# Applying k^T v to q for the later batches: six 32x64 tiles of the matrix array against four 32x128 tiles with a lent PSUM bank

## The chip, the cores and the metric

The kernel runs on one core of a Trainium2 chip. The metric is device time in microseconds, from the run of the whole program; the median of three runs before the change is 1015.61 us (1014.79 to 1016.51). The engines are named as the profile names them: PE is TensorE's matmuls and PEld its weight loads, DVE is VectorE, ACT is ScalarE, POOL is GpSimd, and SP is the engine that issues most DMAs.

## The reference

Two blocks, all in float32. The first is an attention without softmax, over 8 batches, 8 heads, 576 tokens and a head size of 64; the second is a gated feed-forward layer on its output, 4608 tokens of 512 values.

```python
kv = np.einsum('bhsd,bhse->bhde', k, v)
out = np.einsum('bhsd,bhde->bhse', q, kv)
rms = np.sqrt(np.mean(out * out, axis=-1, keepdims=True) + 1e-06)
attn = out / rms * g_norm
x = attn.transpose(0, 2, 1, 3).reshape(B * S, H * D)
gate = 1.0 / (1.0 + np.exp(-(x @ w_gate)))
return gate * (x @ w_val) @ w_out
```

Below, u is the product of q and k^T v (the `out` of the third line), before the norm.

## The kernel before

**Chunks and batches.** The feed-forward layer works in nine chunks of 512 tokens. Chunk 0 is done with plain matmuls while the weights are converted. Chunks 1 to 8 use a fast scheme with fewer products: the first layer (`first_layer_fast`, PE line L949) has 78 products, numbered p = 0 to 77, in three blocks j of 26 (i = p mod 26); the second layer (L1053) has 26. A product of the first layer is two matmuls of a 128x256 moving operand, and each float32 matmul shows as two records in the trace, so it has four records.

**Attention, hidden in the chunks.** Batch 0 is computed before everything else. Batch b (1 to 7) is computed by `feed(b)` while chunk b - 1 runs: its steps are hung behind numbered products, by a list written out by hand for batch 1 (`places`) and lists of pairs (place, step) for batches 2 to 7 (`first`). "At p" below means: right after product p, on each engine behind what that product issued. Each engine works in the order in which instructions were issued to it.

**The steps of a batch.** `kv_mm` (L376, L382) makes k^T v of all heads in PSUM; `kv_copies` (L387) is twelve ACT copies of 32 partitions into `kvq`. q comes in by `load_q`, a pair of heads at a time, on SP's queue, and `turn` (L393) transposes blocks of 32x32 on DVE into `qTs`, on 96 partitions. `two_pairs` then serves four heads: `u_mm` (L422) is 72 matmuls with weights of 32 partitions and 64 columns (64 tokens) from `qTs` and 64 moving columns from `kvq`; six of them that follow each other lie in six places of the array, three row groups by two column halves. They write a three-bank PSUM tile, `at`. `u_square` (ACT, L428) squares u into `sqs`, `u_sum` (DVE, L431) sums, `u_root` (ACT, L434) takes the root, `u_norm` (DVE, L440) divides u, read from PSUM, and `x_turn` (DVE, L447) transposes back and sends the result into the ring `xT` by DMAs on SP (L457). Batch 1 normalizes on ACT instead (`norm`, L463).

**PSUM.** Of the eight banks, `at` holds three. The products of chunks 1 to 8 share the other five through a queue, `free`: a product that opens a new region takes the front bank, and the bank goes to the back when the region's last reader has been issued. Regions are written more than once. The first layer's list starts so (name of the region, two operands, and what `combine` does after the product):

```python
PRODUCTS1 = (("A", 8, 4, ""), ("B", 18, 10, ""), ("C", 9, 1, ""), ("E", 23, 12, "o5=A"), ("A", 24, 14, "o4=C"),
             ("C", 26, 16, "o3=B o1=A"), ("B", 25, 19, "o1=o1+B"), ("A", 33, 9, "t9=E t9=t9+A t8=C"),
```

`o5=A` is an ACT copy of region A (L915). The product i = 4 adds onto A, so on PE it has to wait until that copy has read A; the product i = 5 adds onto C and waits for `o4=C`; the product i = 6 adds onto B and waits for `o3=B`. Sums such as `o1=o1+B` are on DVE (L919). The lines that order all this for one product:

```python
combine(o, regions, steps, nc.vector if j == N3 - 1 and i == NPR - 1 else nc.gpsimd)
give_all(regions, LAST1, i)
for step in at.get(p, ()):
    step()
```

In chunk 1 the first `u_mm` is at p = 25 and the second at p = 53; in chunks 2 to 6 they are at p = 28 and p = 54 (blocks j = 1 and j = 2, behind i = 2). `u_square` of chunks 2 to 6 is at p = 30 and p = 56, behind the copies `o5=A` and `o4=C`.

Of the kernel before, what the change touches and what calls it, by code (L numbers as in the profile page):

```python
# [10 lines left out]
FP32 = mybir.dt.float32  # L11
# [9 lines left out]
def kernel(  # L21
# [30 lines left out]
    NQ = NP // QB  # L52
    QC = QB * NJ
    NC = HD // QB
    XC = QB * JH
# [38 lines left out]
    def load_q(n):  # L94
        if n >= B * NHP:
            return
        b, h0 = n // NHP, 2 * (n % NHP)
        if n < NE:
            t = first.tile([NP, NJ, 2, HD], FP32, tag="q", name="q")
            for e in range(2):  # L100
                nc.sync.dma_start(out=t[:, :, e, :], in_=q[b, h0 + e].rearrange("(p j) d -> p j d", j=NJ))
        else:
            if b == 1:
                i = n - NE
                t = h_main[2 - i // 2].rearrange("p s c -> p (s c)")[0:NP, (i % 2) * 2 * NJ * HD:(i % 2 + 1) * 2 * NJ * HD]
                t = t.rearrange("p (h c) -> p h c", h=2)
            else:
                t = sb.tile([NP, 2, NJ * HD], FP32, tag="q", name="q", bufs=1)
            nc.sync.dma_start(out=t, in_=q[b, h0:h0 + 2].rearrange("h (p j) d -> p h (j d)", j=NJ))
        pairs[n]["q"] = t  # L110
# [147 lines left out]
    kvq = const.tile([P, NHP, 2 * NC, HD], FP32, name="kvq")  # L258

    qTs = const.tile([P, 2, 2 * NJ * HD], FP32, name="qTs")  # L260
    sqs = const.tile([P, 2 * NU * P], FP32, name="sqs")
    xTs = const.tile([P, NC, 2, S // 2], FP32, name="xTs")
# [15 lines left out]
    def attention(n, at_ps):  # L278
# [3 lines left out]
        kv = kvq[:, m, 0]  # L282
# [19 lines left out]
        def q_out():  # L302
            d["qT"] = qTs[:, n % 2, 0:S]
            nc.scalar.copy(out=d["qT"].rearrange("p (i n) -> p i n", i=2), in_=d["q"][:, :, 0:JH * NP])
# [59 lines left out]
    def feed(b):  # L364
# [20 lines left out]
        def kv_copies(i, rs):  # L385
            for r in rs:
                nc.scalar.copy(out=kvq[QB * r:QB * r + QB, :, i].rearrange("p (s n) d -> p s n d", s=2),  # L387
                               in_=d["kv"][QB * i:QB * i + QB])

        def turn(n, e):  # L390

            w_ = NJ * HD
            nc.vector.transpose(qTs[0:NP, n % 2, w_ * e:w_ * e + w_],  # L393
                                pairs[n]["q"][:, e].rearrange("p (j i c) -> p i j c", i=NC, c=QB))
            if e == 1:
                if b > 1:
                    load_q(n + 1)
                elif n == 2 * NHP - 1:
                    load_q(n + 1)

        def two_pairs(n0):


            d = {}
            ms = sb.tile([P, NQ, NJ], FP32, tag="ms2", name="ms2", bufs=1)
            sq = sqs[:, 0:2 * S].rearrange("p (r c) -> p r c", r=NQ)
            units = [slice(NJ // 2 * i, NJ // 2 * (i + 1)) for i in range(2)]

            def by_head(t):
                return t.rearrange("p r (n d) -> p r n d", d=HD)  # L410

            def u_mm(some=range(2)):
                if 0 in some:
                    d["u"] = at_ps()[:, 0:NQ, 0:2 * QC]
                u = d["u"]
                for which in some:
                    for g in range(JH):
                        for i in range(NC):
                            for r in range(NQ):
                                for e in range(2):  # L420
                                    c, o = NJ * HD * e + QC * i + PH * g, HD * (JH * which + g)
                                    nc.tensor.matmul(u[HD * e:HD * e + HD, r, o:o + HD],  # L422
                                                     qTs[QB * r:QB * r + QB, (n0 + which) % 2, c:c + PH],
                                                     kvq[QB * r:QB * r + QB, (n0 + which) % NHP, NC * e + i],
                                                     start=(i == 0), stop=(i == NC - 1))

            def u_square():
                nc.scalar.activation(out=sq, in_=d["u"], func=AF.Square)  # L428

            def u_sum(i):  # L430
                nc.vector.tensor_reduce(out=ms[:, :, units[i]], in_=by_head(sq)[:, :, units[i]], axis=AX.X, op=ALU.add)  # L431
# [4 lines left out]
            def u_norm(i):  # L436
                if i == 0:
                    nc.vector.reciprocal(ms, ms)
                m_ = ms[:, :, units[i]]
                nc.vector.tensor_tensor(out=by_head(sq)[:, :, units[i]], in0=by_head(d["u"])[:, :, units[i]],  # L440
                                        in1=m_.unsqueeze(3).to_broadcast([P, NQ, NJ // 2, HD]), op=ALU.mult)

            def x_turn(i):


                for which in range(2):
                    nc.vector.transpose(xTs[:, i, which],  # L447
                                        sq.rearrange("p r (w g i c) -> p w i r g c", w=2, g=JH, i=NC)[:, which, i])
                m = n0 % NHP
                for j in range(2):  # L450
                    for e in range(2):
                        p0, p1 = HD * e + QB * j, HD * e + QB * i
                        s0 = 0
                        while s0 < S // 2:
                            o = (S * b + S // 2 * j + s0) % (NX * G)
                            n_ = min(NX * G - o, S // 2 - s0)
                            nc.sync.dma_start(out=xT_ring[p1:p1 + QB, m:m + 2, o:o + n_],  # L457
                                                          in_=xTs[p0:p0 + QB, i, :, s0:s0 + n_])
                            s0 += n_

            def norm(r):
                for n in range(NJ):
                    nc.scalar.activation(out=by_head(sq)[:, r, n], in_=by_head(d["u"])[:, r, n], func=AF.Copy,  # L463
                                         scale=ms[:, r, n:n + 1])

            if b == 1:
                u_mms = [lambda: u_mm((0,)), lambda: u_mm((1,))]
                norms = [lambda: nc.vector.reciprocal(ms, ms)] + [lambda r=r: norm(r) for r in range(NQ)]
            else:
                u_mms = [u_mm]  # L470
                norms = [lambda: u_norm(0), lambda: u_norm(1)]
            return (u_mms + [u_square, lambda: u_sum(0), lambda: u_sum(1), u_root] + norms +
                    [lambda i=i: x_turn(i) for i in range(NC)])

        def turns_of(n):
            return [lambda n=n, e=e: turn(n, e) for e in range(2)]

        n0 = NHP * b
        kv = [kv_mm] + [lambda i=i: kv_copies(i, range(3)) for i in range(2 * NC)]
        t0, t1, t2, t3 = (turns_of(n0 + i) for i in range(4))  # L480
        u0, u1 = two_pairs(n0), two_pairs(n0 + 2)
# [700 lines left out]
```

## Time and profile before

| What | Before |
|---|---|
| median of three runs | 1015.61 us (1014.79 to 1016.51) |
| span of the profiled execution | 1013.2 us |
| PE busy | 1003.4 us (99%), 6982 records |
| DVE, ACT, POOL busy | 723.7, 360.2, 591.6 us |
| granted TensorE clock | 1.000 over the span |
| `u_mm` (L422) | 2016 records, 26.4 us busy |
| `kv_copies` (L387) | 84 copies, 30.6 us busy |
| `xT<-xTs` on SP (L457) | 128 DMAs |

The profiled execution lists its span only. The median stands 2.4 us over it, and this is taken as what lies around the span. A row of a group view gives the line, engine, names of the tiles, shapes and count, then busy time and mean time of one; a row of a timeline gives start, duration, engine, line, names and count of merged records, and in brackets the idle time before it and what ended it. A "(x144)" there counts records, two for each float32 matmul.

### The profile page before, as it was taken

What the parts mean: (1) busy time and instruction counts of PE and PEld (TensorE: products, weight loads), DVE (VectorE), ACT (ScalarE), POOL (GpSimd) and SP (SyncE); (2) the same over time, 40 slices, a digit from 0 to 9 for tenths busy, and PEclk for the clock granted to TensorE, in tenths of its full rate; (3) what the DMA queues carried; (4) which work ended last, traced back from release to release, by engine and by line L of the source; (5) the groups of instructions that cost most, each with busy time, mean ns of one, the idle gap of its engine ahead of it and who ended that gap; (6) DMA issues with size and microseconds to landing.
All of it is one profiled execution on the core that took longest, in us unless ns stands there. A gap on an engine that the chain in (4) does not pass through costs nothing.

```text
span 1013.2 us, 18540 instructions
## 1 busy us (share of the span) xinstructions
PE 1003.4 (99%) x6982; PEld 824.1 (81%) x6982; DVE 723.7 (71%) x1215; ACT 360.2 (36%) x639; POOL 591.6 (58%) x965
## 2 busy tenths in 40 slices
PE   9999999999999999999999999999999999999998
PEld 8454447888888888888888888888888888888887
DVE  4888998899668856775677666866688556755672
ACT  4568522442144304441354115421453033213320
POOL 0000999898448642966177706962496439744963
PEclk9999999999999999999999999999999999999999
DMA  9796415644688467646766476556664545444514
GB/s 273 237 282 198 151 43 177 216 137 152 209 272 309 165 192 260 221 160 200 238 230 195 147 248 234 191 164 192 229 217 153 179 155 209 162 154 159 211 58 123
DMA packets 100248, 195.07 MB, mean 193 GB/s; under 512 B 24224, under 2 KB 73248, under 8 KB 100160
## 3 DMA queue, kind: packets, MB, share of 16 engines
q0 software_dynamic: 20976, 112.87, 32.8%
q1 hardware_dynamic: 72016, 78.94, 25.4%
q10 hardware_dynamic: 7168, 2.10, 0.9%
q8 instruction: 55, 0.90, 0.4%
q14 instruction: 33, 0.27, 0.1%
HBM read 160.04 MB, written 25.56 MB: 183 GB/s over the span
## 4 chain that ended last, share of the span: by engine, by line
PE 74%; POOL 2%; issue 0%; DVE 0%; POOLq 0%
PE mm L949 47%; PE mm L1053 24%; PE at L422 2%; PE at L376 1%; POOL h L724 1%; POOL w_ring L1024 0%; POOL h_more L724 0%; PE at L382 0%; POOL w L772 0%; DVE sg L919 0%; POOL w L1024 0%; POOLq L1024 0%
## 5 line engine op out<-in xcount | busy, mean ns | idle before, releaser
L949 PE MATMUL mm<-xs,w 128*128 128x256 f32 x1428 | 332.0, 380 | 0.0
L949 PEld LDWEIGHTS mm<-xs,w 128*128 128x128 f32 x1428 | 270.4, 190 | 37.4 <-DVE temps L919 0.4
L949 PE MATMUL mm<-xT,w 128*128 128x256 f32 x948 | 230.0, 380 | 0.0
L949 PEld LDWEIGHTS mm<-xT,w 128*128 128x128 f32 x948 | 179.4, 190 | 25.5 <-issue 1.0
L919 DVE TENSOR_TENSOR sg<-sg,mm 128x512 f32<-128x512 f32 (+1 forms) x176 | 100.8, 599 | 96.0 <-PE mm L949 45.6
L772 POOL DMA_DIRECT2D w<-kept x84 | 46.9, 558 | 190.8 <-PE mm L949 188.5
L1053 PE MATMUL mm<-w,h 128*128 128x256 f32 x630 | 143.4, 379 | 0.9 <-POOL h L911 0.5
L1053 PEld LDWEIGHTS mm<-w,h 128*128 128x128 f32 x630 | 119.5, 190 | 17.9 <-POOL h L911 0.9
L915 ACT COPY temps<-mm 128x512 f32<-128x512 f32 (+1 forms) x128 | 66.0, 537 | 190.0 <-PE mm L949 94.9
L911 POOL TENSOR_TENSOR h<-h,sg 128x512 f32<-128x512 f32 x72 | 97.7, 1374 | 54.0 <-DVE h L919 33.8
L724 POOL TENSOR_TENSOR h<-h 128x128 f32<-128x128 f32 x216 | 114.0, 540 | 16.5 <-DVE h_more L724 13.1
L1053 PE MATMUL mm<-w,h_more 128*128 128x256 f32 x474 | 108.2, 379 | 0.0
L908 ACT ACTIVATE sg<-sg 128x512 f32<-128x512 f32 x96 | 59.6, 630 | 131.5 <-DVE sg L919 131.5
L1053 PEld LDWEIGHTS mm<-w,h_more 128*128 128x128 f32 x474 | 90.1, 190 | 12.2
L915 ACT COPY sg<-mm 128x512 f32<-128x512 f32 (+1 forms) x112 | 57.1, 510 | 91.2 <-PE mm L1053 45.2
L589 PE MATMUL mm<-xT,w 128*128 128x512 f32 x176 | 78.4, 598 | 1.8 <-ACT xT L352 1.5
L724 POOL TENSOR_TENSOR h_more<-h 128x128 f32<-128x128 f32 x120 | 59.1, 495 | 33.5 <-DVE h L911 29.2
L919 DVE TENSOR_TENSOR temps<-temps,mm 128x512 f32<-128x512 f32 (+1 forms) x96 | 59.2, 617 | 25.8 <-PE mm L1053 17.2
L919 DVE TENSOR_TENSOR temps<-mm,temps 128x512 f32<-128x512 f32 (+1 forms) x64 | 39.8, 622 | 51.0 <-PE mm L1053 23.6
L915 ACT COPY h<-mm 128x512 f32<-128x512 f32 x48 | 28.1, 586 | 125.5 <-PE mm L949 110.3
L743 POOL TENSOR_TENSOR h_more<-w 128x256 f32<-128x256 f32 x10 | 12.1, 1231 | 100.7 <-DMA st<-in_moe_w_out_dram 100.7
L919 DVE TENSOR_TENSOR sg<-mm,sg 128x512 f32<-128x512 f32 (+1 forms) x64 | 39.6, 618 | 43.2 <-PE mm L1053 21.8
(135 smaller groups left out, 1313.6 us busy)
## 6 DMA issues: line engine op xcount, KB each, us to landing
w<-kept POOLq DMA_DIRECT2D x42, 896.0 KB, 5.0
w<-kept POOLq DMA_DIRECT2D x90, 384.0 KB, 4.6
w<-kept POOLq DMA_DIRECT2D x42, 768.0 KB, 5.3
out_dram<-sg SPq DMA_DIRECT2D x119, 64.0 KB, 1.7
h_more<-in_k_dram SPq DMA_DIRECT2D x28, 256.0 KB, 5.0
h_more<-in_v_dram SPq DMA_DIRECT2D x28, 256.0 KB, 5.2
q<-in_q_dram SPq DMA_DIRECT2D x24, 288.0 KB, 3.2
xT<-xTs SPq DMA_DIRECT2D x96, 72.0 KB, 3.9
```

Source lines behind the costliest of these rows:

```text
L376: nc.tensor.matmul(ps[HD * e:HD * e + HD, n // 2, n % 2], mains[n, "k"][:, c], mains[n, "v"][:, c], start=(n % 2 == 0 and j == 0), stop=Fa ...
L422: nc.tensor.matmul(u[HD * e:HD * e + HD, r, o:o + HD], qTs[QB * r:QB * r + QB, (n0 + which) % 2, c:c + PH], kvq[QB * r:QB * r + QB, (n0 + ...
L589: nc.tensor.matmul(self.ps[i], w[("wg", "wv")[i], self.f][:, m, :], xT[self.c][:, m, :], start=(m == 0), stop=(m == NMT - 1), skip_group_c ...
L724: ops.append((eng, lambda v=v, x=x, sign=sign, y=y, eng=eng: eng.tensor_tensor(out=h_form(v, j), in0=h_form(x, j), in1=h_form(y, j), op=op ...
L743: nc.gpsimd.tensor_tensor(out=w1_slot(j, w_at[v]), in0=w1_slot(j, w_at[x]), in1=w1_slot(j, w_at[y]), op=op_of(sign))
L772: nc.gpsimd.dma_start(out=granule(g)[:, 0:n], in_=kept1[g // NPA % N3, g % NPA][:, 0:n])
L908: nc.scalar.activation(out=o["o" + step[1]], in_=o["o" + step[1]], func=AF.Sigmoid)
L911: mult.tensor_tensor(out=o[x], in0=o[x], in1=o[y], op=ALU.mult)
L915: nc.scalar.copy(out=o[out_], in_=o[expr])
L919: tt(out=o[out_], in0=o[x], in1=o[y], op=ALU.add if sign == "+" else ALU.subtract)
L949: nc.tensor.matmul(regions[name][1][:, g], ws[:, g], xf[c][wv], start=(new and g == 0), stop=True, skip_group_check=True)
L1053: nc.tensor.matmul(regions[name][1], h_form(hv, j), ws[:, j], start=(used[i] and j == 0), stop=(j == N3 - 1), skip_group_check=True)
```

## The change

For batches 1 to 7 the four heads of a run lie on 32 partitions each, all 128 partitions in use. q of four heads comes in one DMA (`load_q_run`), and `turn` is two transposes of 128x576 for four heads. `u_mm` takes 128 tokens as weights (32 partitions by 128 columns), in five slices of which the last overlaps the one before, so it has 40 matmuls: for each slice and each half of the head size, four that follow each other, one on each row group. They write four banks: the three of `at`, and one more, which is bank 4 for batch 1 and is taken from the queue `free` for batches 2 to 7. For these, a new step `u_copy` has ACT copy u (960 and 320 values a partition) to `sqs` in SBUF, and the bank is given back to the queue when the copies are issued. `u_square` reads the copy and writes into `qTs`; `u_norm` works in SBUF. `kv_copies` is eight copies of 32x128 a batch. `x_turn` is one transpose of 128x640 per half, with twice the number of DMAs of half the size. Tokens come out in another order, and `store` follows it. The places of the steps are new lists: `u_copy` stands with `u_mm` (p = 25, 53 in chunk 1; 28, 54 in chunks 2 to 6), `u_square` at 26, 55 and 30, 56. In chunks 2 to 6 the turns of q move to p = 4, 8, 33, 39; the norms of the first run are at 42 and 44 and its `x_turn` at 47 and 49.

```diff
+        if b == 1:
+            t = h_main[2 - m].rearrange("p s c -> p (s c)")[:, 4 * NT * P - JR * HD:4 * NT * P]
+        else:
+            t = sb.tile([P, JR * HD], FP32, tag="q", name="q", bufs=1)
+        nc.sync.dma_start(out=t, in_=q[b, HR * m:HR * m + HR].rearrange("h (p j) d -> (h p) (j d)", j=JR))
...
-        def kv_copies(i, rs):
-            for r in rs:
-                nc.scalar.copy(out=kvq[QB * r:QB * r + QB, :, i].rearrange("p (s n) d -> p s n d", s=2),
-                               in_=d["kv"][QB * i:QB * i + QB])
+        def kv_copies(e, i):
+            for r in range(2):
+                p0, p1 = HD * e + QB * i, QB * (2 * r + e)
+                nc.scalar.copy(out=kvq[p1:p1 + QB, :, i], in_=d["kv"][p0:p0 + QB, :, r])
+
+        def turn(m, i):
+            nc.vector.transpose(qTs[:, S * i:S * i + S],
+                                q_late[b, m].rearrange("p (j i c) -> p i j c", i=NC, c=QB)[:, i])
...
+            un = sqs.rearrange("p (h s d) -> p h s d", h=HR, d=HD)
+            sq = un if b == 1 else qTs.rearrange("p (h s d) -> p h s d", h=HR, d=HD)
...
+            def u_mm():
+                d["bank"] = None if b == 1 else free.popleft()
+                more = bank(4 if b == 1 else d["bank"])
+                at = at_ps()
+                d["u"] = [by_slice(at[:, 0:NAT]), by_slice(more.unsqueeze(1))]
+                for s_ in range(NSL):
+                    c = min(P * s_, S - P)
+                    for i in range(NC):
+                        for h in range(HR):
+                            nc.tensor.matmul(d["u"][h // NAT][:, h % NAT, s_],
+                                             qTs[QB * h:QB * h + QB, S * i + c:S * i + c + P],
+                                             kvq[QB * h:QB * h + QB, m, i],
+                                             start=(i == 0), stop=(i == NC - 1))
+
+            def u_copy():
+                nc.scalar.copy(out=un[:, 0:NAT], in_=d["u"][0])
+                nc.scalar.copy(out=un[:, NAT:HR], in_=d["u"][1])
+                give(d["bank"])
...
             def u_square():
-                nc.scalar.activation(out=sq, in_=d["u"], func=AF.Square)
+                if b == 1:
+                    nc.scalar.activation(out=sq[:, 0:NAT], in_=d["u"][0], func=AF.Square)
+                    nc.scalar.activation(out=sq[:, NAT:HR], in_=d["u"][1], func=AF.Square)
+                else:
+                    nc.scalar.activation(out=sq, in_=un, func=AF.Square)
...
+                nc.vector.transpose(xTs[:, i].rearrange("p h c -> p (h c)"),
+                                    sqs.rearrange("p (h s i c) -> p i (h s) c", h=HR, i=NC, c=QB)[:, i])
...
-            return (u_mms + [u_square, lambda: u_sum(0), lambda: u_sum(1), u_root] + norms +
+            return ([u_mm] + ([u_copy] if b > 1 else []) + [u_square, lambda: u_sum(0), lambda: u_sum(1), u_root] + norms +
                     [lambda i=i: x_turn(i) for i in range(NC)])
...
+        names = ("t00 t01 t10 t11 u0 c0 q0 s00 s01 r0 n00 n01 x00 x01 u1 c1 q1 s10 s11 r1 n10 n11").split()
+        steps_ = dict(zip(names, t0 + t1 + u0 + u1[:8]))
+        where = """0:t00 5:t01 25:u0,c0 26:q0 28:s00 30:s01 31:t10 35:t11 42:r0 46:n00 48:n01 50:x00 52:x01 53:u1,c1
+                   55:q1 57:s10,s11 60:r1,n10 62:n11""" if b == 2 else """
+                   4:t00 8:t01 28:u0,c0 30:q0,s00 32:s01 33:t10 37:r0 39:t11 42:n00 44:n01 47:x00 49:x01 54:u1,c1
+                   56:q1,s10,s11 60:r1 61:n10 63:n11"""
...
     def at_ps():
-        return psum.tile([P, NQ, 512], FP32, tag="at", name="at")
+        return psum.tile([P, NAT, 512], FP32, tag="at", name="at")
```

## The prediction

> **What bounds the kernel now.** I read the busy times first, then TensorE's waits, then the groups of small matmuls, then the timelines of PE, ACT and DVE around one `u_mm`.
>
> ```profile
> PE 1003.4 (99%) x6982; PEld 824.1 (81%) x6982; DVE 723.7 (71%) x1215; ACT 360.2 (36%) x639; POOL 591.6 (58%) x965
> ```
>
> The waits of TensorE over the span come to some 6 us, most of it at the start; one of them matters later:
>
> ```profile
> PE mm L949 <- ACT sg L915: 0.8, 1, 0.8
> ```
>
> So PE sets the end: whatever lengthens PE's work, or makes it wait, lengthens the kernel by as much. The groups of small matmuls and weight loads:
>
> ```profile
> L422 PE MATMUL at<-kvq,qTs 32*64 32x64 f32 x2016 | 26.4, 224 | 0.4 <-ACT sqs L463 0.3
> ...
> L949 PEld LDWEIGHTS mm<-xs,w 128*128 128x128 f32 x1428 | 270.4, 190 | 37.4 <-DVE temps L919 0.4
> L422 PEld LDWEIGHTS at<-kvq,qTs 32*64 32x64 f32 x2016 | 24.1, 130 | 7.6 <-issue 5.4 <-ACT sqs L463 1.1 <-ACT cz L206 0.8
> L376 PEld LDWEIGHTS at<-h_more 128*64 128x64 f32 x448 | 13.6, 138 | 3.2 <-issue 2.4 <-ACT sg L594 0.8
> ```
>
> A load of 64 columns takes 130 ns with 32 rows and 138 with 128 rows, one of 128 columns 190: rows hardly count, and 64 more columns cost 52 ns, 0.81 ns a column. The timeline of PE in chunk 2:
>
> ```profile
> 288.05 2.09 PE L376 MATMUL at<-h_more 128*64 128x64 f32 x64
> 290.06 0.46 PE L382 MATMUL at<-h_more 64*64 64x64 f32 x16
> ...
> 294.88 1.03 PE L949 MATMUL mm<-xs,w 128*128 128x256 f32 x4
> 295.74 1.03 PE L949 MATMUL mm<-xT,w 128*128 128x256 f32 x4
> 296.69 1.85 PE L422 MATMUL at<-kvq,qTs 32*64 32x64 f32 x144
> 298.48 4.58 PE L949 MATMUL mm<-xs,w 128*128 128x256 f32 x20
> ```
>
> A product comes every 0.86 us (294.88 to 295.74). With `u_mm` between, the next comes after 2.74, and its first load adds 0.10 (4.58 against 4 x 0.86 + 1.03), so one `u_mm` costs 1.98 us. Of the twelve in chunks 1 to 6 the mean is 1.98. L376's 64 records are 32 rounds of two tiles: (2.09 - 0.27) / 31 = 58.5 ns a round. L382's 16 are four rounds of four tiles in 0.46, the same pace, and the 144 here are 24 rounds of six. A round of 64-column loads thus takes 58.5 ns whatever the number of tiles, and tiles in different rows load side by side. ACT and DVE there:
>
> ```profile
> 296.14 1.24 ACT L915 COPY h<-mm 128x512 f32<-128x512 f32 x2
> 298.58 1.13 ACT L428 ACTIVATE sqs<-at 128x1152 f32<-128x1152 f32 x1 [1.19 <-PE at L422]
> 299.61 0.58 ACT L915 COPY sg<-mm 128x512 f32<-128x512 f32 x1
> ```
>
> ACT makes `o5=A` and `o4=C` (296.14) before `u_mm` ends, then waits for u. In chunk 4, VectorE before the second `u_mm` (536.37):
>
> ```profile
> 531.25 0.26 DVE L438 RECIPROCAL ms<-ms 128x18 f32<-128x18 f32 x1
> 531.54 0.76 DVE L440 TENSOR_TENSOR sqs<-at,ms 128x576 f32<-128x576 f32 x1
> 532.21 0.56 DVE L393 STREAM_TRANSPOSE qTs<-q 96x384 f32<-96x384 f32 x1
> 532.71 0.72 DVE L440 TENSOR_TENSOR sqs<-at,ms 128x576 f32<-128x576 f32 x1
> 533.35 0.67 DVE L919 TENSOR_TENSOR sg<-mm,sg 128x512 f32<-128x512 f32 x1
> ...
> 535.73 0.68 DVE L919 TENSOR_TENSOR h<-mm,temps 128x512 f32<-128x512 f32 x1
> 536.34 1.54 DVE L447 STREAM_TRANSPOSE xTs<-sqs 128x288 f32<-128x288 f32 x4
> ```
>
> VectorE has no gap here. The operation that ends at 536.41 is the last reader of the bank at the front of `free` at that moment.
>
> **The change part by part.**
>
> *`u_mm` on PE.* 40 matmuls in rounds of four, two records each: 20 rounds. Each row group loads 128 columns a round: 0.81 x 128 = 104 ns, plus the 5 to 6 ns by which a 64-column round exceeds its load (58.5 against 53), so 109. Rounds: 20 x 0.109 = 2.18. The rest of `u_mm` (changing over on both sides, the first load) is 0.58 now (1.98 - 24 x 0.0585); L376 with L382, read in the same way, gives 0.50 with one change-over more, of 0.15. I take 0.40, first long load included: 2.58, or 0.60 more each. Twelve: +7.2. In batch 1 each run has two half `u_mm` of 1.18 (62.66 to 63.65 and the edges), and one of 2.58 replaces them: +0.2 each, +0.4. Bounds: a round at the old 58.5 (1.57 in all), and load and move one after the other (0.107 + 0.053 = 0.163 a round, 3.66). The load rows are the nearest, so 109.
>
> *`u_copy` on ACT.* The rows for copies and squares (586 ns for 512 values, 1131 for 1152) give 0.85 ns a value over 150: 968 ns for 960 values, 423 for 320, 1240 for the square; the next may start some 0.105 before an end. In chunks 2 to 6 `u_copy` is issued at p = 28 and 54, ahead of `o5=A` and `o4=C`, and waits for the end of `u_mm`, so both copies, early now, queue behind it. From that end: copies start at 0.03 and 0.89, `o5=A` at 1.21 to 1.80, `o4=C` to 2.28, the square 2.17 to 3.41, `o3=B` 3.30 to 3.89. PE runs product i = 3 from 0.04, then i = 4 would start at 0.89, but writes A: it starts at 1.80 + 0.05, and its load is no longer hidden (0.10): 1.96, a wait of 1.07. Product i = 5 is in time (C read at 2.28, due 2.82); i = 6 needs B, read at 3.89, and would be due at 3.68: 0.37 more. So 1.44 each, ten times: +14.4. In chunk 1, at p = 25, four products stand between and nothing waits; at p = 53 the same sum gives 0.2 and 0.75, less the 0.8 of the wait shown above, which is of this kind and goes: +0.2. Bounds for the ten: 0, and 2.3 each if the square also delayed i = 5.
>
> *The lent bank and VectorE.* The fourth tile of `u_mm` now waits for the front bank's last reader. At p = 28 two turns that stood at p = 24 are gone, and nothing waits. At p = 54 VectorE has, ahead of that reader, a reciprocal, two norms of 640 values (0.75 each, from the 0.76 for 576) and two transposes of 640 (446 ns for 288 and 559 for 384 give 0.86, every 0.80): 3.4 us where 531.25 to 533.35 has 2.1. The reader ends 1.3 later, at 537.7; `u_mm` is due at 536.28 and waits till then: 1.3 in five chunks, +6.5. Bounds: 0 (VectorE catches up) and 2.0.
>
> *Batch 1.* Norms on ACT go from 18 to 20 (one every 0.2), squares from one to two: the wait of the second run for `at` (0.3 now, on L463) grows by some 0.5: +0.5.
>
> *At nothing.* ACT's `kv_copies` (84 of 364 ns, then 56 shorter) end before `u_mm`. Turns are half as many and longer (0.79 for 576 values), beside PE. q's loads: one for two, issued 20 products ahead. DMAs into `xT`: 240 for 128, 0.6 us each on SP; 16 last some 10 us where 8 took 5.9, and behind them SP's stores wait; the sums that read them begin about 12 us after the first, so they end just in time. If that cover failed, each chunk lost 1 to 2 us of VectorE, and the banks there have about 3 us to spare.
>
> *Sum*: 7.2 + 0.4 + 14.4 + 0.2 + 6.5 + 0.5 = +29.2. Against the profiled span: 1013.2 + 29.2 = 1042.4; with the 2.4 around it, **1044.8 us**.
>
> **The rivals.**
>
> *Copies in time (chance 0.15).* PE meets neither ACT's queue nor the bank, only its own work: +8.1, 1023.7. For it: ACT is busy 36%. Against: the order of issue, and the 0.8 wait.
>
> *Short loads (0.10).* The 32x128 load is no slower than the 64-column one: `u_mm` 1.57, so -0.41 x 12 and -0.8 a run in batch 1, -6.5 in all; the other terms stay: +15.1, 1030.7. Against: 190 against 138 ns. The Trainium skill, page "TensorEngine Tiling (Array Packing)", section "Restrictions", says that column tiling shuts off Fast Weight Load, and the change drops column tiling; but the skill's page "TensorE: Matmul & The Clock Gate", section "Weight-path perf modes", gives that mode to weights that are not float32 only. No run so far shows a 32x128 load.
>
> *Load and move in turn (0.06).* A row group cannot load while it multiplies: `u_mm` 3.66, +1.68 x 12 and +2.6 in batch 1; +22.8 and the others' 21.6: 1060. Against: four records of L949, each with a 128-column load of about 0.10 and 256 moving columns, come in 0.86. The Trainium skill, page "TensorE: Matmul & The Clock Gate", section "The mechanism", says that a load overlaps running matmuls only when its row group differs, which would give this rival's time; these four records, all on the full array, disagree.
>
> *Absorbed (0.07), the other side.* PE is not the true bound of a chunk, and what it loses in the first layer comes back at the layers' ends, where it would otherwise wait for POOL's sums of h. Price nil: 1015.6, the median of before. It decides if a chunk can give back 29.2 / 6 = 4.9 us. Against: in chunks 1 to 6 (182 to 812 us) PE is busy 628.25 of 630.
>
> **How the numbers follow.** The forecast has 0.62 and by itself 1035 to 1053, from its three bounds taken by halves. 1022 to 1054 takes in the first two rivals and leaves out some 2 in 10, the last two with the tails. 0.2% is 2 us, about what a measurement of this kernel can tell from no change. Faster 0.03 and same 0.03 are the last rival's, with 0.01 slower; slower 0.94.
>
> **What would show it.** `u_mm` as 1120 records in about 2.6 us each, with loads near 184 ns; `PE mm L949` waiting for ACT's copies at L921 of the changed file (`h`, then `sg`), ten times near 1.1 and ten near 0.4; PE in `u_mm` waiting for DVE's `h` once a chunk. Wrong, if `u_mm` stays at or under 2 us, if PE has no wait at i = 4, or if PE's idle time grows by less than 10 us.

## The result and the profile after

The changed kernel takes 1042.6 us (median of four runs, 1042.15 to 1043.99) against 1015.2 of the kernel before: a ratio of 1.0269, 95% interval 1.0256 to 1.0281. The span of its profiled execution is 1040.7 us against 1013.2, so 27.5 us have to be found. Times below are medians of four runs too, but for `order_all`: one run of it took 3787.8 us, which nothing here explains, and its time is the median of the other three. The busy times of the page:

```profile
PE 1019.1 (98%) x6086; PEld 830.8 (80%) x6086; DVE 720.2 (69%) x1159; ACT 358.6 (34%) x641; POOL 593.2 (57%) x965
```

PE is busy 15.7 us longer with 896 records fewer, and the rest is time in which it stands still. What it stands still for (reason, us in total, times, longest):

```profile
PE mm L955 <- ACT h L921: 8.1, 11, 0.8
...
PE mm L425 <- DVE h L925: 1.4, 5, 0.3
...
PE mm L955 <- DVE sg L925: 0.9, 1, 0.9
```

L955, L921 and L925 are L949, L915 and L919 of before, and L425 is the new `u_mm`. These sums are too small, since products overlap: the next is due 0.16 us before the record of the one ahead ends (0.97 behind its start, where the row lasts 1.13), and the load that a wait lays bare costs 0.10 more. So I took the starts of the products in both traces (both have 3744 records of the first and second layer, in the same order) and subtracted: how much later does product p + 1 start after product p than it did before?

| Place | Before to after, us | How often | Sum, us |
|---|---|---|---|
| `u_mm` itself (the product behind it) | 2.74 to 3.35: 0.61 | 12 | 7.3 |
| i = 4 and its load, behind the first `u_mm` | 0.98 + 0.10 | 5 | 5.4 |
| i = 4 and its load, behind the second | 0.84 + 0.10 | 5 | 4.7 |
| i = 6 and its load, behind both | 0.30 + 0.10 | 10 | 4.0 |
| second `u_mm`, beyond the 0.61 | 0.76 in four chunks, 0.40 in chunk 4 | 5 | 3.4 |
| product p = 50 and its load | 0.23 in four chunks, 1.21 in chunk 2 | 5 | 2.1 |
| chunk 1, the rest (0.58 of it at p = 78, the first product of the second layer, a wait for POOL) | | 1 | 0.5 |
| batch 1 (0.1), start (-0.25), small ones (0.3), end (-0.2) | | | -0.1 |
| sum (of 27.5) | | | 27.3 |

Elsewhere products start as far apart as before; chunks 7 and 8, in which no attention runs, have no difference at all.

The groups of `u_mm` by tile, from the view of that line (duration least, median, greatest in ns; then the forms):

```profile
L425 PE MATMUL at<-kvq,qTs x840: 270/270/318, 62.4 to 779.1; 32*128 32x64 f32 x168
L425 PE MATMUL mm<-kvq,qTs x280: 270/270/318, 62.4 to 779.3; 32*128 32x64 f32 x140
```

```profile
L425 PEld LDWEIGHTS at<-kvq,qTs x840: 181/187/187, 62.4 to 779.1; 32*128 32x128 f32 x168
```

A load of 32 rows and 128 columns takes 187 ns, within 3 ns of the 190 of a 128x128 load before. The starts of the 80 records of one `u_mm` come as 7, 6, 7, then 92 ns: four records close together, then a pause, 111 or 112 ns a round (160 for the first).

PE and ACT behind the first `u_mm` of chunk 2 (start, duration, engine, line):

```profile
300.79 1.13 PE L955 MATMUL mm<-xs,w 128*128 128x256 f32 x4
302.74 4.12 PE L955 MATMUL mm<-xs,w 128*128 128x256 f32 x16 [0.82 <-ACT h L921]
```

```profile
300.91 0.96 ACT L431 COPY sqs<-at 128x960 f32<-128x960 f32 x1 [4.27 <-PE mm L425]
301.76 0.43 ACT L432 COPY sqs<-mm 128x320 f32<-128x320 f32 x1
302.08 1.09 ACT L921 COPY h<-mm 128x512 f32<-128x512 f32 x2
303.04 1.30 ACT L440 ACTIVATE qTs<-sqs 128x1280 f32<-128x1280 f32 x1
304.21 1.09 ACT L921 COPY sg<-mm 128x512 f32<-128x512 f32 x2
```

ACT waits 4.27 us for `u_mm` with `o5=A` and `o4=C` queued behind the copies (the x2 at 302.08), and `o3=B` (304.21) behind the square. Product i = 3 starts at 300.79, i = 4 at 302.74, just after the first of the two has read A. The 16 records from there take 4.12 us, 0.5 more than four products that follow each other without a wait: 0.10 is the load that the wait at i = 4 laid bare, 0.40 is i = 6 with its load.

VectorE and PE around the second `u_mm` of chunk 2:

```profile
322.28 0.84 DVE L456 STREAM_TRANSPOSE xTs<-sqs 128x640 f32<-128x640 f32 x1
323.04 0.65 DVE L925 TENSOR_TENSOR sg<-mm,sg 128x512 f32<-128x512 f32 x1
323.62 0.82 DVE L456 STREAM_TRANSPOSE xTs<-sqs 128x640 f32<-128x640 f32 x1
...
326.13 0.68 DVE L925 TENSOR_TENSOR h<-mm,temps 128x512 f32<-128x512 f32 x1
```

```profile
321.62 1.13 PE L955 MATMUL mm<-xs,w 128*128 128x256 f32 x4 [0.95 <-DVE sg L925]
...
326.87 0.32 PE L425 MATMUL mm<-kvq,qTs 32*128 32x64 f32 x1 [0.28 <-DVE h L925]
```

The fourth tile, in the lent bank, starts when the sum at 326.13 has ended. And a product five places earlier, p = 50, already waits for a sum that VectorE does late.

### The profile page after: what moved, and what is told of

Same layout as the page of the kernel before. It is cut to its first block, busy times and chain, and to the rows that moved or that the text cites. A ratio compares the mean times of both kernels' runs of the same rounds, so it can differ in the third digit from the quotient of the medians.

```text
span 1040.7 us, 16813 instructions
## 1 busy us (share of the span) xinstructions
PE 1019.1 (98%) x6086; PEld 830.8 (80%) x6086; DVE 720.2 (69%) x1159; ACT 358.6 (34%) x641; POOL 593.2 (57%) x965
## 4 chain that ended last, share of the span: by engine, by line
PE 66%; DVE 4%; ACT 4%; issue 1%; POOL 1%; DMA 0%; ACTq 0%; DVEq 0%; POOLq 0%
PE mm L955 39%; PE mm L1059 24%; PE at L425 1%; DVE h L925 1%; DVE sg L925 1%; PE mm L425 1%; PE at L382 1%; ACT sqs L431 1%; DVE xTs L456 1%; ACT h L921 1%; ACT qTs L440 1%; ACT sg L921 1%; POOL h L728 1%; DVE temps L925 0%; ACT sqs L432 0%
## 5 line engine op out<-in xcount | busy, mean ns | idle before, releaser
L955 PE MATMUL mm<-xs,w 128*128 128x256 f32 x1428 | 338.6, 382 | 9.9 <-ACT h L921 7.5
L955 PEld LDWEIGHTS mm<-xs,w 128*128 128x128 f32 x1428 | 268.3, 190 | 55.9 <-ACT h L921 11.5
L955 PE MATMUL mm<-xT,w 128*128 128x256 f32 x948 | 229.8, 380 | 0.0
L955 PEld LDWEIGHTS mm<-xT,w 128*128 128x128 f32 x948 | 179.2, 190 | 25.4 <-issue 0.5
L925 DVE TENSOR_TENSOR sg<-sg,mm 128x512 f32<-128x512 f32 (+1 forms) x176 | 101.3, 600 | 80.5 <-PE mm L955 38.7
L921 ACT COPY temps<-mm 128x512 f32<-128x512 f32 (+1 forms) x128 | 66.5, 545 | 186.8 <-PE mm L1059 94.7
L917 POOL TENSOR_TENSOR h<-h,sg 128x512 f32<-128x512 f32 x72 | 95.4, 1343 | 57.4 <-DVE h L925 31.3
L921 ACT COPY sg<-mm 128x512 f32<-128x512 f32 (+1 forms) x112 | 56.4, 517 | 86.3 <-PE mm L1059 45.2
L925 DVE TENSOR_TENSOR temps<-temps,mm 128x512 f32<-128x512 f32 (+1 forms) x96 | 59.3, 617 | 24.9 <-PE mm L1059 17.1
L925 DVE TENSOR_TENSOR temps<-mm,temps 128x512 f32<-128x512 f32 (+1 forms) x64 | 39.8, 621 | 47.9 <-PE mm L1059 23.6
L925 DVE TENSOR_TENSOR sg<-mm,sg 128x512 f32<-128x512 f32 (+1 forms) x64 | 39.5, 617 | 42.7 <-PE mm L955 22.6
L747 POOL TENSOR_TENSOR h_more<-w 128x256 f32<-128x256 f32 x10 | 10.3, 1048 | 100.5 <-PE at L382 100.5
L921 ACT COPY h<-mm 128x512 f32<-128x512 f32 x48 | 27.3, 596 | 113.7 <-PE mm L955 113.7
```

The costliest lines, as they stand in the source:

```text
L917: mult.tensor_tensor(out=o[x], in0=o[x], in1=o[y], op=ALU.mult)
L921: nc.scalar.copy(out=o[out_], in_=o[expr])
L925: tt(out=o[out_], in0=o[x], in1=o[y], op=ALU.add if sign == "+" else ALU.subtract)
L955: nc.tensor.matmul(regions[name][1][:, g], ws[:, g], xf[c][wv], start=(new and g == 0), stop=True, skip_group_check=True)
```

## The experiments

The theory has three parts: rounds of `u_mm` last as long as the load of one row group's columns; copies of u in front of `o5=A` and `o4=C` make products wait that nothing else delays; and VectorE is too full between p = 40 and 54, so that the readers of its banks are late. The rivals are that ACT or VectorE simply have too much to do wherever it stands, and that `u_mm` is slow for the number of its records or for coming back to the same row groups. Unless something else is said, an experiment starts from the changed kernel, and "the list" is that of chunks 2 to 6. Ratios are against the kernel before, with 95% intervals.

**copy_late: `u_copy` behind the copies that products wait for.**

```diff
-                   4:t00 8:t01 28:u0,c0 30:q0,s00 ... 54:u1,c1
-                   56:q1,s10,s11 60:r1 61:n10 63:n11
+                   4:t00 8:t01 28:u0 30:c0,q0,s00 ... 54:u1
+                   56:c1,q1,s10,s11 60:r1 61:n10 63:n11
```

> The changed kernel with `u_copy` behind `o5=A` and `o4=C` in chunks 2 to 6 (p = 30 and 56, not 28 and 54). Theory (order of ACT's queue): the wait at i = 4 goes, 0.98 + 0.10 us and 0.84 + 0.10 us a chunk, 10.1 us in five chunks; the 0.40 at i = 6 stays, since copies and square still stand ahead of `o3=B`. 1042.6 - 10.1 = 1032.5 us. Rival (it is the amount of ACT's work, or PSUM being read while PE writes it, and not the order): the same work is done, so no change, 1042.6.

1034.6 us, ratio 1.0187 (1.0171 to 1.0202). ACT and PE in chunk 2:

```profile
298.50 0.58 ACT L921 COPY h<-mm 128x512 f32<-128x512 f32 x1 [1.14 <-PE mm L955]
300.90 0.96 ACT L431 COPY sqs<-at 128x960 f32<-128x960 f32 x1 [1.82 <-PE mm L425]
301.76 0.43 ACT L432 COPY sqs<-mm 128x320 f32<-128x320 f32 x1
302.22 1.27 ACT L440 ACTIVATE qTs<-sqs 128x1280 f32<-128x1280 f32 x1
303.40 1.05 ACT L921 COPY sg<-mm 128x512 f32<-128x512 f32 x2
```

```profile
300.78 2.86 PE L955 MATMUL mm<-xs,w 128*128 128x256 f32 x12
304.02 1.99 PE L955 MATMUL mm<-xs,w 128*128 128x256 f32 x8 [0.38 <-ACT sg L921]
```

`o4=C` starts at 298.50, 2.4 us before the copies of u, and products i = 3 to 5 now run through. The two waits at i = 4 are gone to the hundredth (0.98 + 0.10 and 0.84 + 0.10). Of the 10.1 us 1.7 come back, since i = 6 starts its wait earlier and now waits 0.24 and 0.10 longer for `o3=B`, behind the square. The amount of ACT's work is the same, so it is the order.

**square_early: the same fault, put alone into the kernel before.**

```diff
-  ((3, 0), (7, 1), (24, 2), (24, 3), (28, 8), (28, 4), (30, 5), (30, 9), ..., (54, 17), (56, 18), ...
+  ((3, 0), (7, 1), (24, 2), (24, 3), (28, 8), (28, 9), (28, 4), (30, 5), ..., (54, 17), (54, 18), ...
```

> The kernel before, with one thing alone: in chunks 2 to 6 `u_square` stands right behind `u_mm` (p = 28 and 54, not 30 and 56), so that ACT waits for `u_mm` with `o5=A` and `o4=C` behind it. No copy, no lent bank, the old `u_mm`. Theory (order of ACT's queue): o5=A ends 1.13 + 0.58 after `u_mm`, i = 4 is due at 0.89 and starts near 1.75, its load no longer hidden (0.10): 0.95 a time, ten times, +9.5 us: 1024.7. Nothing at i = 6. Rival (the stall needs the copies or the lent bank): no change, 1015.2.

1025.5 us, ratio 1.0095 (1.0080 to 1.0111): 10.3 us slower than the kernel before, for a step that was moved by two places.

```profile
299.69 1.13 ACT L428 ACTIVATE sqs<-at 128x1152 f32<-128x1152 f32 x1 [2.46 <-PE at L422]
300.72 1.07 ACT L915 COPY h<-mm 128x512 f32<-128x512 f32 x2
```

```profile
299.59 1.13 PE L949 MATMUL mm<-xs,w 128*128 128x256 f32 x4
301.35 1.99 PE L949 MATMUL mm<-xs,w 128*128 128x256 f32 x8 [0.64 <-ACT h L915]
```

Each i = 4 starts 0.80 to 0.91 later and the next 0.10: 9.4 us in ten places. (The profiled execution has a wait of 1.4 us for a load of v at its start besides, which has nothing to do with this.) The stall needs neither the copies nor the lent bank.

**halves: two tiles of 64 columns for one of 128.**

```diff
-                            nc.tensor.matmul(d["u"][h // NAT][:, h % NAT, s_],
-                                             qTs[QB * h:QB * h + QB, S * i + c:S * i + c + P],
+                            for e in range(2):
+                                nc.tensor.matmul(d["u"][h // NAT][HD * e:HD * e + HD, h % NAT, s_],
+                                                 qTs[QB * h:QB * h + QB, S * i + c + HD * e:S * i + c + HD * e + HD],
```

> The changed kernel with each matmul of `u_mm` split into two of 64 weight columns, side by side in the two column halves: 80 matmuls in 20 rounds of eight, the same data and results. Theory (a round lasts as long as the load of one row group's columns): rounds of 0.0585 us in place of 0.112, so u_mm costs 0.35 + 1.17 = 1.52 and not 2.59; 12 x 1.07 = 12.8 us in chunks 1 to 6, up to 2 us more in batch 1: 1028 to 1030 us. Rival 1 (each row group is loaded and multiplied in turn, or the round has a pace of its own): no change, 1042.6, or slower with twice the records. Rival 2 (a price per matmul, (1.98 - 0.58) / 72 = 19 ns from the kernel before): 0.35 + 1.56 = 1.91, 12 x 0.68 = 8 us less, 1034.5.

1041.7 us, ratio 1.0258 (1.0238 to 1.0277), and more spread than others (1039.7 to 1044.3). The time alone is that of rival 1, but `u_mm` is not unchanged: the first one of chunks 2 to 4 costs 2.06 us, 0.53 less than in the change, where the theory gave 1.07 and the price per record (rival 2) 0.68. In chunk 2 the second and third round of eight take 58 ns each, with records 6 to 7 ns apart, as the theory has it. The later ones take 66 to 167 ns, most of their records 8 to 9 or 16 to 17 ns apart, and the mean behind the first round is 84. So the loads (131 ns, as short as before) and the row groups allow rounds of 58 ns; what makes the later records come late was not tested. Most of the gain of 6 us was lost again: this kernel's PE has waits that no kernel with 40 matmuls showed,

```profile
PE at L426 <- issue: 2.1, 2, 1.8
```

and after the longest, in chunk 6, the granted clock is 0.87 and 0.78 in the two stretches of 5 us from 775 on, and 1.00 in those before and behind them. The profile puts down to issue what it sees no other cause for; why these waits come was not tested, and the last section returns to them.

**half_rounds: 64 columns, but one tile a row group in each round.**

```diff
-                for s_ in range(NSL):
-                    c = min(P * s_, S - P)
+                for e, s_ in [(e, s_) for e in range(2) for s_ in range(NSL)]:
+                    c = min(P * s_, S - P) + HD * e
```

> The changed kernel with 64 weight columns a matmul, as in the run `halves`, but all the lower column halves first and then all the upper ones: 160 records in 40 rounds of four, each round coming back to the same row groups and columns. Theory (a round lasts as long as the load of one tile's columns, unless the records themselves take longer, about 10.4 us per 1000): 40 x 0.0585 = 2.34, u_mm 2.69 and not 2.59: 1042.6 + 14 x 0.1 = 1044. Rival 1 (a price per record alone): 160 x 0.0104 + 0.4 = 2.06 as in `halves`, 14 x 0.53 less, 1035. Rival 2 (a fixed price of 0.112 for each return to a row group, whatever the columns): 40 x 0.112 = 4.48, 14 x 2.24 more, 1074.

1046.7 us, ratio 1.0308 (1.0292 to 1.0323). In chunks 2 to 4 the first `u_mm` takes what it took in the change, 2.59 us, with twice the records (prediction 2.69). Starts come as 7, 6, 7, 38 ns: 58 ns a round, where 128 columns make 112.

```profile
L425 PEld LDWEIGHTS at<-kvq,qTs x1680: 127/133/133, 62.0 to 783.0; 32*64 32x64 f32 x187
```

So the record count (rival 1, 2.06) and a fixed price of coming back (rival 2, 4.83) are both out: with four tiles a round it is the columns of the load. With eight the records come too slowly for that. The 4 us above the change are again waits for issue in chunks 5 and 6 (2.4 us in `u_mm`, `PE at L425 <- issue`), and behind the longest, in chunk 6, a lower clock (0.86 and 0.80 in the two stretches of 5 us from 780 on).

**norm_early and turn_early: VectorE's work moved.**

```diff
-  33:t10 37:r0 39:t11 42:n00 44:n01 47:x00 49:x01
+  33:t10 35:r0 38:n00 39:t11 40:n01 43:x00 45:x01        (norm_early)
+  30:t10,t11,q0,s00 32:s01 37:r0 42:n00 44:n01 47:x00 49:x01        (turn_early; its first squares go to xTs)
```

> The changed kernel with the first run's root at p = 35 (was 37), norms at 38 and 40 (were 42, 44) and `x_turn` at 43 and 45 (were 47, 49) in chunks 2 to 6. Theory (VectorE's backlog keeps the lent bank's last reader): VectorE's idle 0.73 us before p = 42 is filled, the reader ends by so much earlier, and the wait in the second `u_mm` (0.71 to 0.76 us, five chunks) goes, with the 0.24 us a chunk at p = 50 (1.2 in chunk 2): 3.5 to 5.5 us less, 1037 to 1039 us. Rival (VectorE is simply full there, or the wait is for another bank's reader): no change, 1042.6.

> The changed kernel with the two turns of the second run (0.77 us of VectorE each) at p = 30 in place of 33 and 39 in chunks 2 to 6, where VectorE is idle; for that the first run's squares go into `xTs` and not into `qTs`. Theory (VectorE's backlog from p = 40 to 54 is more than fits, so work has to leave that stretch, not move within it): the waits at p = 50 (0.24, 1.2 in chunk 2) and at the lent bank (0.71 + 0.05) go; 0.2 comes back at the next wait for ACT: 5 us less in five chunks, 1037.6. Rival (the waits have nothing to do with how much VectorE has to do there): no change, 1042.6.

Neither moved the time: 1042.8 us, ratio 1.0267 (1.0250 to 1.0285), and 1042.9, ratio 1.0271 (1.0256 to 1.0286). In `norm_early` the wait in the second `u_mm` did go, all 0.71 of it, and others took its place: 0.23 at p = 45 and 0.50 more at p = 50 in chunks 3 to 6, and 0.20 at the next wait for ACT. The waits of PE there:

```profile
PE mm L955 <- ACT h L921: 9.1, 11, 0.9
PE mm L955 <- DVE sg L925: 2.7, 5, 0.8
```

In `turn_early` the wait for the lent bank is unchanged to the hundredth (4.05 us from p = 54 to 55), and of the waits at p = 50 only that of chunk 2 shrank, by 0.62; 0.57 more at the start and 0.28 in chunk 5 took that up in the profiled execution. VectorE there has idle gaps up to 313.96, the last while it waits for ACT's copy at p = 40, and none from there to the lent bank's reader, which ends at 326.58:

```profile
313.96 0.70 DVE L925 TENSOR_TENSOR sg<-sg,temps 128x512 f32<-128x512 f32 x1 [0.72 <-ACT sg L921]
...
325.90 0.68 DVE L925 TENSOR_TENSOR h<-mm,temps 128x512 f32<-128x512 f32 x1
```

The turns had stood before that point, so taking them away lengthened the gaps. The backlog begins at p = 40, and my expectation for `turn_early` had its place wrong. In the stretch from p = 40 stand a reciprocal, two norms and two transposes, 3.6 us that PE must wait for at one product or another.

**order_all and order_nine: copies at p = 30 and 56, squares at 31 and 57, turns as in turn_early; then also 72 matmuls.** In `order_nine` the matmuls from batch 2 on are those of `halves` without the half slice that is computed twice (`for e in range(0 if s_ < NSL - 1 or b == 1 else 1, 2)`), and the copies leave that half out.

> As `turn_early`, and `u_copy` behind `o4=C` (p = 30, 56) and `u_square` behind `o3=B` (p = 31, 57) in chunks 2 to 6; the matmuls as in the change. Theory: all waits of these chunks go and only the longer `u_mm` is left, 12 x 0.61 = 7.3 us, with about 1 us in chunk 1: 1015.2 + 8.3 = 1023.5. Rival (the order of ACT's queue was only part of it and the copies still delay `o3=B`): 0.4 a run more, 1027.5.

> As `order_all`, and from batch 2 on the matmuls split as in `halves`, without the half slice that was computed twice: 72 matmuls, 144 records. Theory: 144 x 0.0104 + 0.39 = 1.89 a `u_mm` and not 2.59; ten of them, against 1.98 before: 0.9 less than before, batch 2 in chunk 1 included, and 0.6 more in chunk 1: 1014.9, no different from before by what this can tell. Rival (the waits for the issue of instructions that `halves` showed in chunks 1 and 6 come here as well): 2 to 4 us more, 1018.

1036.6 us, ratio 1.0211 (1.0191 to 1.0232), and 1034.3, ratio 1.0184 (1.0169 to 1.0199): both far above theory and rival. In `order_all` all waits at i = 4 and i = 6 are gone, in all ten places. But squares of 1.3 us now stand ahead of `t8=C`, and product p = 34 (60 in the second) waits 0.38 + 0.10 for it; and the lent bank's wait is still there. Part of the expectation failed for that, and part since VectorE's wait was counted as gone with `turn_early`. In `order_nine` the first `u_mm` takes 1.95 us, as little as before the change (1.98), but most of what this saves is lost elsewhere: in chunks 3 to 6 p = 34 loses 0.77, p = 60 some 0.86, p = 50 0.76 and the second `u_mm` 0.3 to 0.7, and chunk 2 has a wait for issue of 2.0 us. Its expectation counted waits as gone that were still there.

**order2 and order3: VectorE's first norms ahead of p = 40, squares on VectorE.**

```diff
+  4:t00 8:t01 28:u0 30:c0,t10,t11 31:q0 32:s00 33:s01 35:r0 36:n00 38:n01 47:x00 50:x01 54:u1 56:c1 59:q1 60:s10,s11 62:r1 63:n10 65:n11   (order2)
+  ... 34:r0 36:n00 38:n01 47:x00 50:x01 54:u1 56:c1 57:q1 58:s10 59:s11 60:r1 61:n10 63:n11   (order3)
+                    nc.vector.tensor_tensor(out=sq, in0=un, in1=un, op=ALU.mult)
```

In order2 the square of the first run is on VectorE, in order3 both (chunks 2 to 6); order2 also changes chunk 1's list, order3 has that of the change. "All" has the 40 matmuls of 128 columns, "nine" the 72 of 64 from batch 2 on.

> As `order_all`, and in chunks 2 to 6 the norms of the first run at p = 36 and 38 (were 42, 44), its root at 35, its `x_turn` at 47 and 50; the first run's squares on VectorE (idle there) and the second run's on ACT at p = 59, behind `t8=C`. Matmuls as in the change. Theory (in `order_all` VectorE has no gap from the sum at p = 40 to the lent bank's reader; only work taken out of that stretch helps, and the turns that `turn_early` moved had stood before it; the squares on ACT held `t8=C`): all these waits go, and what is left is 12 x 0.61 for the longer `u_mm` and about 0.6 in chunk 1: 1023.5. Rival (VectorE's waits come back at other products, as in `norm_early`): order_all less the 5 us at `t8=C`, 1031.

> As `order2_all`, with the 72 matmuls of `order_nine` from batch 2 on, whose `u_mm` cost 1.98 us there, as before the change. Theory: 1015.2, with 1 to 3 us for the waits for issue that `order_nine` showed (2.7 us in two places): 1015 to 1018. Rival (as above): 1024.

> As `order2_nine`, with chunk 1's list as in the change again (the new one cost 4 us there, in sums held back from p = 62 on), and in chunks 2 to 6 the first root at p = 34, ahead of the copy `t0=F`, and the second run's squares on VectorE too, at p = 57. Theory (what is left in `order2_nine` is VectorE: a norm that starts late because the root stands behind a copy on ACT, 1 us a chunk at p = 42, and the second run's norms, 0.2 to 0.5 a chunk at p = 68): span 1026.3 - 4 - 5 - 2 = 1015, time 1017.5. Rival (VectorE has no room for the squares and the waits come back at other products): no better than 1028.3 less the 4 us of chunk 1, 1024.

> As `order3_nine`, with the matmuls of the change (40 of 128 weight columns): the change with its waits taken away as far as these lists do it. Theory (the longer `u_mm` and the waits add up): in chunks 3 to 5 each `u_mm` costs 0.61 more than before the change, with 0.1 to 0.5 a chunk besides, and no wait for the issue of instructions: 12 x 0.61 = 7.3, chunk 1's 0.6 at p = 78, some 1.5 for VectorE: span 1013.2 + 9.4 = 1022.6, time 1025. Rival (with 128 columns the longer `u_mm` gives VectorE and ACT the time that they lack, so the terms do not add): no slower than `order3_nine` without its waits for issue, 1021.

| Kernel | Time, us | Ratio (95%) |
|---|---|---|
| order2_all | 1034.3 | 1.0178 (1.0151 to 1.0206) |
| order2_nine | 1028.3 | 1.0113 (1.0082 to 1.0144) |
| order3_nine | 1023.8 | 1.0080 (1.0063 to 1.0097) |
| order3_all | 1032.2 | 1.0171 (1.0154 to 1.0188) |

None came out at the theory's number; `order3_nine` came out at its rival's (1024), and both order2 kernels above theirs (1031 and 1024). Order2's new list for chunk 1 alone costs 4.1 us (5.8 lost there, against 1.7 in the change). In `order3_nine` chunks 3, 4 and 5 do come within 0.8, 0.1 and 0.5 us of the kernel before: all of ACT's waits and nearly all of VectorE's are gone there. What that kernel still loses is 3.9 us in chunk 2 (1.8 of it a wait for issue), 3.8 in chunk 6 and 1.7 in chunk 1. In `order3_all` the same list with the longer `u_mm` should have cost 1.2 us a chunk more, and cost 2.2 to 3.3 more in chunks 3 to 5. Most of the difference goes back to one instruction. VectorE, POOL and PE of `order3_all` in chunk 3:

```profile
446.27 2.01 DVE L454 TENSOR_TENSOR sqs<-sqs,ms 128x640 f32<-128x640 f32 x1
448.21 0.68 DVE L927 TENSOR_TENSOR temps<-mm,temps 128x512 f32<-128x512 f32 x1
```

```profile
446.32 1.28 POOL L730 TENSOR_TENSOR h<-h 128x128 f32<-128x128 f32 x3
447.67 0.93 POOL L730 TENSOR_TENSOR h_more<-h 128x128 f32<-128x128 f32 x1
```

```profile
448.94 2.86 PE L957 MATMUL mm<-xs,w 128*128 128x256 f32 x12 [1.00 <-DVE temps L927]
```

A norm that takes 0.82 us when POOL is idle took 2.01 beside POOL's sums, and the product at p = 69 waited for the sum behind it: 1.16 to 1.28 us in four chunks. In `order3_nine` the same norm takes 1.07 us in chunks 3 to 5, and 2.03 in chunk 6, where p = 69 loses 1.48. So the terms do not add: what shifts one engine decides whether two others meet. None of these versions beats the kernel before.

## Why the prediction was right, point by point

*That PE bounds and that nothing is absorbed*: right. Chunks 1 to 6 lose 27.9 us, chunks 7 and 8 gain nothing back.

*`u_mm` on PE*: 2.58 predicted, 2.59 measured; 12 x 0.61 = 7.3 against 7.2. The rule behind it, that a round lasts as long as its load, is what `half_rounds` shows. That the two numbers are so close is in part luck: a round is 112 ns, not 109, and the rest 0.35, not 0.40. One sentence holds only for part of the rounds: that one of 64 columns takes 58.5 ns "whatever the number of tiles". In the first `u_mm` of chunk 2 before the change 15 of 23 rounds of six take 58 or 59 ns, the first 106 and the other seven 65 to 96, and with eight tiles the mean is 84 (`halves`). The row that the prediction shows does not give 58.5 either: 1.85 us for 24 rounds, less 0.22 for the last record, is 71 ns for each of the 23. The rivals of short loads (load 187 ns, not 130) and of load and move in turn (0.112 a round, not 0.163) are both refuted by the rows. The price of the latter was added up wrongly: 0.107 + 0.053 is 0.160, which gives 3.60 a `u_mm`.

*`u_copy` on ACT*: 1.07 + 0.37 predicted, ten times, 14.4. Measured 1.08 + 0.40 behind the first and 0.94 + 0.40 behind the second `u_mm`, 14.1. The mechanism is shown from both sides by `copy_late` and `square_early`. The rival that the copies come in time is refuted.

*The lent bank and VectorE*: the place and the engine were right, the size was not. 6.5 was predicted, 1.3 a chunk (its own times, 537.7 and 536.28, give 1.4); 3.4 was measured. Two things were missed. In chunk 4 the step was 0.37 longer than in the other chunks before the change too, most of it a wait for issue inside `u_mm`, and the bank's wait stands in its place (the step goes from 3.05 to 4.05 us, 0.61 of it the longer `u_mm`). And some of the lateness is paid earlier: product p = 50 loses 0.23 a chunk (1.21 in chunk 2), which pushes PE back before it comes to the lent bank. Both together are 5.6 us; the rest of the 6.5 is not explained. That VectorE's lateness moves from product to product but stays is what `norm_early` shows.

*Batch 1*: +0.4 and +0.5 predicted, +0.1 measured. One long `u_mm` costs 1.02 to 1.41 us more than the half that it replaces, and the other half's 1.07 to 1.18 goes. The wait on the squares, which was to grow by 0.5, went away with its 0.3. That term was wrong.

*Chunk 1's copies*: +0.2 predicted, -0.1 measured around the second `u_mm`; 0.58 at p = 78, a wait for POOL's sum of h, was not foreseen.

*At nothing*: turns, q's loads and the DMAs into `xT` cost PE nothing that the table shows in chunks 2 to 6. Left out of that list was that `u_norm` now has both operands in SBUF; the last section says what that does.

The sum was 29.2 for 27.5: 3.1 too much at the lent bank and 0.8 in batch 1, 2.1 too little at p = 50 and 0.3 in chunk 1, the others within 0.3. That the sum is only 1.7 off is in part luck, since errors of opposite sign cancel. And what lies around the span is 1.8 us in the runs of both kernels (1042.5 against 1040.7), not the 2.4 that the forecast added.

## What to carry to other kernels

An instruction that waits on an in-order engine charges its wait to everything queued behind it: before moving a step earlier, list what was issued behind it and who waits for that. Narrow matmuls have two floors, the columns of the load of one row group and the pace at which records come (10 to 11 ns each over a whole `u_mm` here), and the larger one is the price; fewer and wider tiles can cost more than many narrow ones. An engine with no gap cannot be relieved by moving its work within the full stretch; find where the backlog begins, and move work to before that point.

## What the runs showed of the hardware that I had not expected

*VectorE slows beside POOL when both its operands are in SBUF.* The norm of before reads u from PSUM, that of the change from SBUF. Durations (least, median, greatest) from the views of that line, of the kernel before, the changed kernel and `order3_all`:

```profile
L440 DVE TENSOR_TENSOR sqs<-at,ms x24: 714/754/758, 206.1 to 762.9; 128x576 f32<-128x576 f32 x24
```

```profile
L452 DVE TENSOR_TENSOR sqs<-sqs,ms x24: 818/918/1989, 204.9 to 790.6; 128x640 f32<-128x640 f32 x24
```

```profile
L454 DVE TENSOR_TENSOR sqs<-sqs,ms x24: 820/1116/2031, 205.0 to 780.3; 128x640 f32<-128x640 f32 x24
```

All 24 of the first had sums of POOL's beside them, and none took more than 0.76 us; the second takes 0.82 us in the nine cases in which no sum of POOL's runs at the same time, and up to 1.99 when one does. The sums of 512 values at L925 of the changed kernel, from 182 to 812 us, say the same: 276 that read a PSUM bank take 0.69 us at most, with POOL or without; of those in SBUF alone the 53 away from POOL's sums take 0.69 at most, and of the 33 beside them 16 take 0.75 to 2.04. Where VectorE is not slowed, POOL is: beside ten of the other 17 POOL's sum of h took 1.31 to 1.66 us, where it takes 1.26 at the least. So one of the two waits for the other. The Trainium skill, page "SBUF — State Buffer", section "Who interferes with whom", says that a VectorE instruction with two SBUF inputs contends with a GpSimd instruction that reads SBUF, and one with at most one SBUF input does not; these rows agree. In chunk 2 of the changed kernel the first norm (1.11 for 0.82) and two sums (0.94 and 1.08 for 0.68) are slowed so, 0.95 us together, which is about what p = 50 loses more in that chunk (1.21) than in the others (0.23). In `turn_early` the norm took 0.82 and the second sum 0.94, and p = 50 lost 0.60 in that chunk. That fits, but its turns had moved too; no run tested the cause alone.

*Many records in a row come at 10 to 11 ns each.* Behind the first round the 160 records of `halves` came at 10.5 ns and the 144 of the kernel before at 10.4 to 10.8, in a `u_mm` without a longer wait, on four row groups and on three. This is a mean, not a price of each: within a round the first 28 (32 in `halves`) came 6 to 7 ns apart, the later ones mostly 8 to 9 or 16 to 17. The Trainium skill, page "TensorE: Matmul & The Clock Gate", section "Measured speedup vs the span model", has some 4 ns a tile, and by that the eight tiles of `halves` would have hidden behind their loads; measured, they did so in two of 19 rounds. The same page, section "LDWEIGHTS (loading the stationary operand)", has the load's time as columns / 1.2 ns, the same for 32 rows as for 128: 107 ns for 128 columns and 53 for 64, and the rounds of 112 and 58 ns agree, both with 5 ns on top.

*Left open*: what the waits for issue inside `u_mm` come from, 1.8 to 2.7 us in `halves`, `half_rounds`, `order_nine` and `order3_nine`, all with 64-column tiles in the new layout. `order2_nine` has such tiles and shows none on PE; the kernel before has 144 records in each `u_mm` too and shows only a short one, in chunk 4 (two records 0.28 us apart at 538.2). The traces point to the loading of PE's instructions: each of the nine waits over 0.3 us ends 2.2 to 2.7 us after the start of a 16 KB transfer on the queue q8, which the profile calls "instruction", and there is about one such transfer for 126 records of PE (55 before the change, 48 after it). No run tested this.
